# Attention plus gated FFN on one core: K's weights moved to another DMA queue, two crossbar tiles ranked earlier, one PSUM copy moved to ScalarE

## The chip, the cores and the metric

One core of a Trainium2 chip. The metric is the device time of one execution in us; smaller is better. The kernel before takes 517.59 us (median of 3 runs, 517.06 to 518.33).

## The reference, cut to what matters

```python
x = A_x                                  # (1, 2048, 576) bf16
xn = _layernorm(x)                       # mean, variance over 576
# A: linear attention, 32 heads of 18
qkv = xn @ wqkv                          # (576, 3*576)
phi = lambda t: where(t > 0, t + 1, exp(t)) + 1e-6
kv  = einsum("bhsd,bhse->bhde", phi(k), v);  z = sum over s of phi(k)
o   = (phi(q) @ kv) / (phi(q) . z + 1e-6) @ wo
# B: gated FFN, 4608 wide
return x + o + (gelu(xn @ w_gate) * (xn @ w_up)) @ w_down
```

The 2048 rows are 16 tiles of 128. The first stage (up to 70 us) makes, for each tile, the layernorm, its transpose, the K and Q projections, phi of both, and the sums G = xn^T phi(K). The rest (446 us) is mostly the FFN.

## The kernel before, the parts concerned

Loads at the start. SyncE and ScalarE each issue DMAs on a queue of their own (q1 and q10 in the profile):

```python
def load_w(which, on=nc.sync):           # which: 0 = Q, 1 = K, 2 = V
    c = slice(which * D, (which + 1) * D)
    on.dma_start(wqkv_sb[:, 0:4, c], A_wqkv[0:512, c].rearrange("(kt p) c -> p kt c", p=P))
    on.dma_start(wqkv_sb[0:HP, 4, c], A_wqkv[512:576, c])      # the tail, 64 rows

load_x(0, 1)                             # tile 0, SyncE
load_x(1, 1, nc.scalar)                  # tile 1, ScalarE
load_w(1, nc.scalar)                     # K
nc.scalar.preload_act_table_set("natural_log_exp_and_others")
load_x(2, 2)                             # tiles 2, 3
load_w(0)                                # Q
load_x(4, 4)
```

Tiles 0 and 1 are transposed by TensorE into PSUM and copied out; tiles 2 to 15 go through the DMA crossbar:

```python
def transposes(n, k0=0, k1=KT, b=None):  # TensorE
    for kt in range(k0, k1):
        nc.tensor.transpose(tp_bank(b)[:, kt, :], xn[:, n, kt * P:(kt + 1) * P], ident[:])
def dma_transposes(n):                   # DMA crossbar
    nc.sync.dma_start_transpose(xnT[:, :, n * P:(n + 1) * P], xn[:, n, 0:640])
```

A planner in the program fixes the order of instructions at build time. Each step has an engine, an assumed duration, a rank, the steps it needs, a `ready` time for loads and a `tail` until its result lands. It starts what can start earliest, and among what can start within 0.05 us takes the lowest rank. None of these numbers is work on the chip; they only order the instructions.

```python
X_AT = [3.50, 4.20, 6.50, 6.50] + [9.50] * 4
for n in range(NS):
    lead = {0: -9.0, 1: 0.5}.get(n, 0.0)
    ...
    step(("stats", n, h), "DVE", 0.41, n - 2.2 + lead, ...)
    step(("aggr", n), "DVE", 0.21, n - 2.1 + lead, ...)
    step(("rstd", n), "ACT", 0.49, n - 2.1 + lead, ...)
    if n < TD:                           # TD = 2: transposed by TensorE
        for i, (k0, k1, eng) in enumerate([(0, 3, "ACT"), (3, KT, "DVE")]):
            step(("norm", n, i), "DVE", ...); step(("tp", n, i), "PE", ...)
            step(("xnT", n, i), eng, 0.48 if eng == "ACT" else 0.30, n - 0.88 + lead, ...)
    else:                                # crossbar
        step(("norm", n), ...)           # ScalarE for odd tiles, VectorE for even ones
        step(("xnT", n), "SP", 2.10, n - 1.9, [("norm", n)], lambda n=n: dma_transposes(n), tail=0.6)
    # mm, exp, phi of K (rank n) and Q (rank n + 0.6) in halves; G (rank n + 1.15)
```

Of the kernel before, what the change touches and what calls it, by code (L numbers as in the profile page):

```python
# [8 lines left out]
ACT = mybir.ActivationFunctionType  # L9
# [6 lines left out]
P = 128  # L16
HP = 64
# [11 lines left out]
KT = 5  # L29
# [28 lines left out]
def kernel(  # L58
# [11 lines left out]
    nc = tc.nc  # L70
# [21 lines left out]
    def load_x(n0, cnt, on=nc.sync):  # L92
        on.dma_start(x_sb[:, n0:n0 + cnt, :], x_view[:, n0:n0 + cnt, :])
# [8 lines left out]
    wqkv_sb = apool.tile([P, KT, 3 * D], BF16, name="wqkv_sb")  # L102


    def load_w(which, on=nc.sync):
        c = slice(which * D, (which + 1) * D)
        on.dma_start(wqkv_sb[:, 0:4, c], A_wqkv[0:512, c].rearrange("(kt p) c -> p kt c", p=P))  # L107
        on.dma_start(wqkv_sb[0:HP, 4, c], A_wqkv[512:576, c])

    load_x(0, 1)  # L110
    load_x(1, 1, nc.scalar)
    load_w(1, nc.scalar)
    nc.scalar.preload_act_table_set("natural_log_exp_and_others")
    load_x(2, 2)
    load_w(0)
    load_x(4, 4)

# [18 lines left out]
    xnT = persist.tile([P, KT, S], BF16, name="xnT")  # L136
# [63 lines left out]
    def ln_half(n, h):  # L200
        if h == 0:
            ln_raw[n] = asmall.tile([P, 2, nc.vector.BN_STATS_DIM], F32, name="stats")
        nc.vector.bn_stats(out=ln_raw[n][:, h, :], in_=x_sb[:, n, h * HALF:(h + 1) * HALF])  # L203

    def ln_aggr(n):
        nc.vector.bn_aggr(out=mv[:, n, :], in_=ln_raw[n][:])

    def ln_rstd(n):
        r = rstd[:, n:n + 1]
        nc.scalar.activation(out=r, in_=mv[:, n, 1:2], func=ACT.Ln, bias=eps_ln[:], scale=1.0)  # L210
        nc.scalar.activation(out=r, in_=r, func=ACT.Exp, scale=-0.5)

    def ln_bias(n):
        nc.gpsimd.tensor_scalar(
            out=nbias[:, n:n + 1], in0=mv[:, n, 0:1], scalar1=rstd[:, n:n + 1], scalar2=-1.0, op0=ALU.mult, op1=ALU.mult,
        )

    def ln_norm_act(n):
        nc.scalar.activation(  # L219
            out=xn[:, n, 0:D], in_=x_sb[:, n, :], func=ACT.Identity, bias=nbias[:, n:n + 1], scale=rstd[:, n:n + 1],  # L220
        )

    def ln_norm(n, c0=0, c1=D):
        nc.vector.tensor_scalar(
            out=xn[:, n, c0:c1], in0=x_sb[:, n, c0:c1], scalar1=mv[:, n, 0:1], scalar2=rstd[:, n:n + 1],
            op0=ALU.subtract, op1=ALU.mult,
        )
# [8 lines left out]
    def transposes(n, k0=0, k1=KT, b=None):  # L236
        b = TP_BANK[n] if b is None else b
        for kt in range(k0, k1):
            nc.tensor.transpose(tp_bank(b)[:, kt, :], xn[:, n, kt * P:(kt + 1) * P], ident[:])

    def tp_copy(n, k0=0, k1=KT, b=None, copy=acopy):
        b = TP_BANK[n] if b is None else b
        copy(out=xnT[:, k0:k1, n * P:(n + 1) * P], in_=tp_bank(b)[:, k0:k1, :])

    def dma_transposes(n):
        nc.sync.dma_start_transpose(xnT[:, :, n * P:(n + 1) * P], xn[:, n, 0:640])
# [4 lines left out]
    def kq_mm(n, which, hf):  # L251
        c = which * D + hf * HALF
        for kt in range(KT):
            nc.tensor.matmul(  # L254
                ps_all[:, KQ_BANK[which] + hf, :HALF], lhsT=xnT[:, kt, n * P:(n + 1) * P],
                rhs=wqkv_sb[:, kt, c:c + HALF], start=(kt == 0), stop=(kt == KT - 1),
            )

    def kq_exp(n, which, hf):
        e = e_tiles[n, which, hf] = awork.tile([P, HALF], F32, name="phi_e", tag="phi_e", bufs=8)  # L260
        nc.scalar.activation(  # L261
            out=e[:], in_=ps_all[:, KQ_BANK[which] + hf, :HALF], func=ACT.Exp, bias=neg1[:], scale=1.0,
        )

    def kq_phi(n, which, hf):
        nc.vector.scalar_tensor_tensor(  # L266
            out=(pq, pk)[which][:, n, hf * HALF:(hf + 1) * HALF], in0=e_tiles[n, which, hf][:], scalar=1.0,
            in1=ps_all[:, KQ_BANK[which] + hf, :HALF], op0=ALU.min, op1=ALU.max,
        )
# [11 lines left out]
    def g_accumulate(n, pieces):  # L281
        for kt, ps_ in pieces.items():
            j0, m = (kt * P, P) if kt < 4 else (4 * P, HP + 1)
            for b, col, d0, w in ps_:
                nc.tensor.matmul(  # L285
                    ps_all[:m, b, col:col + w], lhsT=xn[:, n, j0:j0 + m], rhs=pk[:, n, d0:d0 + w],
                    start=(n == 0 and col == 0), stop=(n == NS - 1), skip_group_check=True,
                )
# [120 lines left out]
    def step(name, *args, **kw):  # L409
        steps[name] = _Step(*args, **kw)  # L410

    X_AT = [3.50, 4.20, 6.50, 6.50] + [9.50] * 4
    W_AT = {1: 5.50, 0: 7.60}

    for n0 in range(8, NS, 2):
        step(("x", n0), "SP", 0.50, n0 - 5.5, [], lambda n0=n0: load_x(n0, 2), ready=1.6 * n0 + 2.0, tail=3.0)
    for n in range(NS):
        lead = {0: -9.0, 1: 0.5}.get(n, 0.0)
        after_x = [("x", n // 2 * 2)] if n >= 8 else []
        x_at = X_AT[n] if n < 8 else 0.0  # L420
        for h in range(2):
            step(("stats", n, h), "DVE", 0.41, n - 2.2 + lead, after_x, lambda n=n, h=h: ln_half(n, h), ready=x_at)
        step(("aggr", n), "DVE", 0.21, n - 2.1 + lead, [("stats", n, 0), ("stats", n, 1)], lambda n=n: ln_aggr(n))
        step(("rstd", n), "ACT", 0.49, n - 2.1 + lead, [("aggr", n)], lambda n=n: ln_rstd(n))
        if n < TD:
            for i, (k0, k1, eng) in enumerate([(0, 3, "ACT"), (3, KT, "DVE")]):
                b = TP_BANK[n] - i
                step(("norm", n, i), "DVE", 0.25, n - 2.1 + lead, [("rstd", n)],
                     lambda n=n, k0=k0, k1=k1: ln_norm(n, k0 * P, min(k1 * P, D)))
                step(("tp", n, i), "PE", 0.20, n - 1.5 + lead, [("norm", n, i)],  # L430
                     lambda n=n, k0=k0, k1=k1, b=b: transposes(n, k0, k1, b))
                step(("xnT", n, i), eng, 0.48 if eng == "ACT" else 0.30, n - 0.88 + lead, [("tp", n, i)],
                     lambda n=n, k0=k0, k1=k1, b=b, eng=eng: tp_copy(n, k0, k1, b, acopy if eng == "ACT" else vcopy))
            ready = [("xnT", n, 0), ("xnT", n, 1)]
        else:
            if n % 2:
                step(("bias", n), "POOL", 0.15, n - 2.1, [("rstd", n)], lambda n=n: ln_bias(n))
                step(("norm", n), "ACT", 0.65, n - 2.1, [("bias", n)], lambda n=n: ln_norm_act(n))
            else:
                step(("norm", n), "DVE", 0.43, n - 2.1, [("rstd", n)], lambda n=n: ln_norm(n))  # L440
            step(("xnT", n), "SP", 2.10, n - 1.9, [("norm", n)], lambda n=n: dma_transposes(n), tail=0.6)
            ready = [("xnT", n)]
        for which, rank in ((1, n), (0, n + 0.6)):
            for h in range(2):
                r = rank + h / 100
                free = [("phi", n - 1, which, h)] if n else []
                step(("mm", n, which, h), "PE", 0.615, r, ready + free, lambda n=n, w=which, h=h: kq_mm(n, w, h),
                     ready=W_AT[which], tail=0.15)
                step(("exp", n, which, h), "ACT", 0.49, r + 0.10, [("mm", n, which, h)],
                     lambda n=n, w=which, h=h: kq_exp(n, w, h))  # L450
                step(("phi", n, which, h), "DVE", 0.44, r + 0.15, [("exp", n, which, h)],
                     lambda n=n, w=which, h=h: kq_phi(n, w, h))
        step(("G", n), "PE", 0.75, n + 1.15, [("phi", n, 1, 0), ("phi", n, 1, 1)], lambda n=n: g_accumulate(n, G_A))
# [42 lines left out]


    load_w(2)
    for i in range(NWBUF):
        load_gu(i, 0)  # L500
# [156 lines left out]
```

## Time and profile before

| | before |
|---|---|
| time, median of 3 | 517.59 us |
| span of the profiled run | 516.2 us |
| TensorE busy | 509.0 us (99%) |
| VectorE, ScalarE busy | 203.4, 136.9 us |
| first K matmul (L254) | 6.73 us |
| FFN's first matmul (L309) | 69.94 us |

TensorE's busy time says little, since matmuls overlap and their ends are modelled. What is read are starts: a step between two groups that is longer than the number of matmuls times their pace is a gap in which TensorE issued nothing. The prediction shows the lines of the TensorE timeline and of the chain of waits.

### The profile page before, as it was taken

The numbers are of one execution on the slowest core, as the hardware profiler recorded it, in microseconds if no ns is written. First come the engines' busy times: TensorE is split into PE (matmuls) and PEld (weight loads), VectorE is DVE, ScalarE is ACT, GpSimd is POOL, SyncE is SP. The second block draws the span as 40 slices with busy tenths as digits, with TensorE's granted clock in tenths as the row PEclk, the third lists the DMA queues.
The fourth block names the chain that finished last, engine by engine and source line by source line (L and its number), as shares of the span: only waits on it lengthen the run. The fifth ranks groups of instructions, "written<-read, shape, count | busy, mean of one in ns | idle before, by whom it ended". The sixth has DMA issues, their size and how long they took to land.

```text
span 516.2 us, 10568 instructions
## 1 busy us (share of the span) xinstructions
PE 509.0 (99%) x4487; PEld 308.6 (60%) x4487; DVE 203.4 (39%) x415; ACT 136.9 (27%) x266; POOL 8.3 (2%) x26
## 2 busy tenths in 40 slices
PE   7999999999999999999999999999999999999997
PEld 6778864444487744444677644444777544445775
DVE  6887447667501036766401133333101234333100
ACT  4888523223310023233100022322000133232000
POOL 3001000000000000000000000000000000000000
PEclk9999999999999999999999999999999999999999
DMA  7443919999900045666400155555100455540000
GB/s 206 103 96 65 251 39 224 286 285 270 235 30 13 13 141 149 175 181 166 133 11 20 55 154 158 158 143 156 33 15 13 126 157 144 158 120 2 13 11 24
DMA packets 118745, 61.02 MB, mean 118 GB/s; under 512 B 25514, under 2 KB 117866, under 8 KB 118698
## 3 DMA queue, kind: packets, MB, share of 16 engines
q1 hardware_dynamic: 117946, 59.54, 44.5%
q8 instruction: 35, 0.57, 0.5%
q10 hardware_dynamic: 752, 0.81, 0.5%
q14 instruction: 12, 0.10, 0.1%
HBM read 52.79 MB, written 2.36 MB: 107 GB/s over the span
## 4 chain that ended last, share of the span: by engine, by line
PE 95%; DMA 3%; ACT 1%; DVE 0%; ACTq 0%; issue 0%; SPq 0%
PE ps_all L309 54%; PE ps_all L604 27%; PE ps_all L254 6%; PE ps_all L609 4%; PE ps_all L285 3%; DMA xnT<-xn 2%; DMA wqkv_sb<-in_A_wqkv_dram 1%; ACT phi_e L261 0%; PE ps_all L356 0%; PE ps_all L586 0%; ACT xn L219 0%; DVE hT L576 0%; ACT gl L575 0%; DVE res L612 0%; ACTq L107 0%
## 5 line engine op out<-in xcount | busy, mean ns | idle before, releaser
L309 PE MATMUL ps_all<-xnT,wg 64*128 64x512 bf16 x1152 | 272.0, 376 | 0.0
L309 PE MATMUL ps_all<-xnT,wu 64*128 64x512 bf16 x1152 | 271.5, 376 | 0.0
L575 ACT ACTIVATE gl<-ps_all 128x512 f32<-128x512 f32 x144 | 86.0, 597 | 313.7 <-PE ps_all L309 313.7
L576 DVE TENSOR_TENSOR hT<-ps_all,gl 128x512 bf16<-128x512 f32 x144 | 99.2, 689 | 143.6 <-ACT gl L575 143.2
L309 PEld LDWEIGHTS <-wu 64*128 64x128 bf16 x1152 | 108.3, 94 | 68.2
L309 PEld LDWEIGHTS <-wg 64*128 64x128 bf16 x1152 | 108.3, 94 | 67.8
L604 PE MATMUL ps_all<-wd_sb,hT 128*128 128x288 bf16 x1152 | 147.1, 286 | 0.0
L604 PEld LDWEIGHTS <-hT 128*128 128x128 bf16 x1152 | 112.3, 98 | 30.0 <-issue 1.6
L612 DVE TENSOR_TENSOR res<-ps_all,x_sb 128x288 bf16<-128x288 f32 x32 | 14.6, 457 | 144.9 <-PE ps_all L609 144.9
L309 PE MATMUL ps_all<-xnT,wr 64*128 64x512 bf16 x288 | 54.7, 376 | 0.0
L254 PE MATMUL ps_all<-wqkv_sb,xnT 128*128 128x288 bf16 x320 | 42.5, 286 | 1.8 <-DMA xnT<-xn 1.0
L254 PEld LDWEIGHTS <-xnT 128*128 128x128 bf16 x320 | 30.3, 98 | 9.8 <-DMA xnT<-xn 1.7
L261 ACT ACTIVATE phi_e<-ps_all,neg 128x288 f32<-128x288 f32 x64 | 30.9, 496 | 10.5 <-PE ps_all L254 7.2
L609 PE MATMUL ps_all<-m_sb,pqT 126*128 126x288 bf16 (+1 forms) x160 | 24.9, 286 | 0.0
L309 PEld LDWEIGHTS <-wr 64*128 64x128 bf16 x288 | 14.0, 94 | 17.3 <-issue 0.7
L285 PE MATMUL ps_all<-hT,xn 128*128 128x288 bf16 (+4 forms) x176 | 22.6, 275 | 0.0
L285 PEld LDWEIGHTS <-xn 128*128 128x128 bf16 (+1 forms) x176 | 17.6, 101 | 3.9
L609 PEld LDWEIGHTS <-pqT 126*128 126x128 bf16 (+1 forms) x160 | 15.6, 97 | 4.1
L266 DVE SCALAR_TENSOR_TENSOR pq<-phi_e,ps_all 128x288 bf16<-128x288 f32 x32 | 14.1, 450 | 8.0 <-ACT phi_e L261 7.8
L266 DVE SCALAR_TENSOR_TENSOR hT<-phi_e,ps_all 128x288 bf16<-128x288 f32 x32 | 14.1, 448 | 3.4 <-ACT phi_e L261 3.3
L203 DVE BATCH_NORM_STATS2 stats<-x_sb 128x6 f32<-128x288 bf16 x32 | 13.5, 439 | 1.8 <-DMA x_sb<-in_A_x_dram 1.8
L388 DVE SCALAR_TENSOR_TENSOR pn<-pq,den_d 128x504 bf16<-128x504 bf16 (+1 forms) x32 | 13.1, 449 | 0.0
(52 smaller groups left out, 95.4 us busy)
## 6 DMA issues: line engine op xcount, KB each, us to landing
wg<-in_B_w_gate_dram SPq DMA_DIRECT2D x72, 256.0 KB, 2.9
wu<-in_B_w_up_dram SPq DMA_DIRECT2D x72, 256.0 KB, 3.5
wd_sb<-in_B_w_down_dram SPq DMA_DIRECT2D x12, 432.0 KB, 5.2
wr<-in_B_w_gate_dram SPq DMA_DIRECT2D x72, 32.0 KB, 2.7
wr<-in_B_w_up_dram SPq DMA_DIRECT2D x72, 32.0 KB, 3.1
out_dram<-res SPq DMA_DIRECT2D x15, 144.0 KB, 1.8
x_sb<-in_A_x_dram SPq DMA_DIRECT2D x5, 288.0 KB, 3.2
wqkv_sb<-in_A_wqkv_dram SPq DMA_DIRECT2D x2, 576.0 KB, 6.7
```

The source lines that it names most:

```text
L203: nc.vector.bn_stats(out=ln_raw[n][:, h, :], in_=x_sb[:, n, h * HALF:(h + 1) * HALF])
L254: nc.tensor.matmul(ps_all[:, KQ_BANK[which] + hf, :HALF], lhsT=xnT[:, kt, n * P:(n + 1) * P], rhs=wqkv_sb[:, kt, c:c + HALF], start=(kt == ...
L261: nc.scalar.activation(out=e[:], in_=ps_all[:, KQ_BANK[which] + hf, :HALF], func=ACT.Exp, bias=neg1[:], scale=1.0,)
L266: nc.vector.scalar_tensor_tensor(out=(pq, pk)[which][:, n, hf * HALF:(hf + 1) * HALF], in0=e_tiles[n, which, hf][:], scalar=1.0, in1=ps_al ...
L285: nc.tensor.matmul(ps_all[:m, b, col:col + w], lhsT=xn[:, n, j0:j0 + m], rhs=pk[:, n, d0:d0 + w], start=(n == 0 and col == 0), stop=(n == ...
L309: return nc.tensor.matmul(self.outs[i], lhsT=self.lhs(i, rows, kt), rhs=self.rhs(i, rows, kt), start=start, stop=stop, skip_group_check=True,)
L388: nc.vector.scalar_tensor_tensor(out=pn[:].rearrange("p (c t) -> p c t", t=P)[:, c0:c1, :nh * DH].rearrange("p c (h e) -> p c h e", e=DH), ...
L575: nc.scalar.activation(out=gl[:], in_=ps_all[:, b[0], :], func=ACT.Gelu_apprx_tanh)
L576: nc.vector.tensor_tensor(out=hT[:, GUB * k + i, :], in0=ps_all[:, b[1], :], in1=gl[:], op=ALU.mult)
L604: nc.tensor.matmul(acc, lhsT=hT[:, f, j * P:(j + 1) * P], rhs=wd_sb[:, f, hs], start=(f == 0), stop=False,)
L609: nc.tensor.matmul(acc, lhsT=pqT[:rows, c, ts_], rhs=m_sb[:rows, c, hs], start=False, stop=(c == NCH - 1),)
L612: nc.vector.tensor_tensor(out=res[:, hs], in0=acc, in1=x_sb[:, n, hs], op=ALU.add)
```

## The change

Its intent: let K's weights have the DMA engines to themselves right after the first tile, bring tile 2 to the crossbar sooner, and take a copy off VectorE, which is the fuller engine at the start.

```diff
-    def load_w(which, on=nc.sync):
+    def load_w(which):                        # always on SyncE's queue
     load_x(0, 1)
     load_x(1, 1, nc.scalar)
-    load_w(1, nc.scalar)
     nc.scalar.preload_act_table_set("natural_log_exp_and_others")
+    load_w(1)
     load_x(2, 2)
     load_w(0)
     load_x(4, 4)
@@
-    X_AT = [3.50, 4.20, 6.50, 6.50] + [9.50] * 4
+    X_AT = [3.65, 4.20, 6.40, 6.40] + [9.50] * 4
-        lead = {0: -9.0, 1: 0.5}.get(n, 0.0)
+        lead = {0: -9.0, 1: 0.5, 2: -0.5, 3: -0.5}.get(n, 0.0)
-            for i, (k0, k1, eng) in enumerate([(0, 3, "ACT"), (3, KT, "DVE")]):
+            for i, (k0, k1, eng) in enumerate([(0, 3, "ACT"), (3, KT, "ACT" if n else "DVE")]):
-                step(("xnT", n, i), eng, 0.48 if eng == "ACT" else 0.30, n - 0.88 + lead, ...
+                step(("xnT", n, i), eng, 0.30 if i else 0.48, n - 0.88 + lead, ...
-            step(("xnT", n), "SP", 2.10, n - 1.9, ..., tail=0.6)
+            step(("xnT", n), "SP", 2.10, n - 1.9, ..., tail=1.7)
```

More of the change, by code (lines that the diff above doesn't have):

```diff
@@ L102 @@
     wqkv_sb = apool.tile([P, KT, 3 * D], BF16, name="wqkv_sb")
-    def load_w(which, on=nc.sync):
+    def load_w(which):
         c = slice(which * D, (which + 1) * D)
-        on.dma_start(wqkv_sb[:, 0:4, c], A_wqkv[0:512, c].rearrange("(kt p) c -> p kt c", p=P))
-        on.dma_start(wqkv_sb[0:HP, 4, c], A_wqkv[512:576, c])
+        nc.sync.dma_start(wqkv_sb[:, 0:4, c], A_wqkv[0:512, c].rearrange("(kt p) c -> p kt c", p=P))
+        nc.sync.dma_start(wqkv_sb[0:HP, 4, c], A_wqkv[512:576, c])
     load_x(0, 1)
     load_x(1, 1, nc.scalar)
-    load_w(1, nc.scalar)
     nc.scalar.preload_act_table_set("natural_log_exp_and_others")
+    load_w(1)
     load_x(2, 2)
@@ L431 @@
                      lambda n=n, k0=k0, k1=k1, b=b: transposes(n, k0, k1, b))
-                step(("xnT", n, i), eng, 0.48 if eng == "ACT" else 0.30, n - 0.88 + lead, [("tp", n, i)],
+                step(("xnT", n, i), eng, 0.30 if i else 0.48, n - 0.88 + lead, [("tp", n, i)],
                      lambda n=n, k0=k0, k1=k1, b=b, eng=eng: tp_copy(n, k0, k1, b, acopy if eng == "ACT" else vcopy))
@@ L440 @@
                 step(("norm", n), "DVE", 0.43, n - 2.1, [("rstd", n)], lambda n=n: ln_norm(n))
-            step(("xnT", n), "SP", 2.10, n - 1.9, [("norm", n)], lambda n=n: dma_transposes(n), tail=0.6)
+            step(("xnT", n), "SP", 2.10, n - 1.9, [("norm", n)], lambda n=n: dma_transposes(n), tail=1.7)
             ready = [("xnT", n)]
```

## The prediction

> **What bounds the kernel now.** I read the page first: TensorE is busy 509.0 of 516.2 us and the chain that ended last is 95% TensorE, 3% DMA, 1% ScalarE. So only stretches in which TensorE issues nothing can be won, and they are few. I looked for them in the TensorE timeline of the first 60 us (start, duration, engine, line, operation, count, and in brackets the idle time with its releaser).
>
> ```profile
> 6.73 0.66 PE L254 MATMUL ps_all<-wqkv_sb,xnT 128*128 128x288 bf16 x4 [0.28 <-ACT xnT L243]
> 7.83 0.91 PE L254 MATMUL ps_all<-wqkv_sb,xnT 128*128 128x288 bf16 x6 [0.44 <-DMA wqkv_sb<-in_A_wqkv_dram]
> 8.57 0.44 PE L239 MATMUL ps_all<-ident,xn 128*128 128x128 bf16 x5
> 8.86 1.39 PE L254 MATMUL ps_all<-wqkv_sb,xnT 128*128 128x288 bf16 x10
> 10.08 0.91 PE L285 MATMUL ps_all<-hT,xn 128*128 128x288 bf16 x7
> 10.82 2.61 PE L254 MATMUL ps_all<-wqkv_sb,xnT 128*128 128x288 bf16 x20
> 14.40 1.40 PE L254 MATMUL ps_all<-wqkv_sb,xnT 128*128 128x288 bf16 x10 [0.96 <-DMA xnT<-xn]
> ...
> 29.17 2.92 PE L254 MATMUL ps_all<-wqkv_sb,xnT 128*128 128x288 bf16 x20
> 31.93 0.91 PE L285 MATMUL ps_all<-hT,xn 128*128 128x288 bf16 x7
> 32.68 2.61 PE L254 MATMUL ps_all<-wqkv_sb,xnT 128*128 128x288 bf16 x20
> ```
>
> The reader is to see starts, not ends (the ends are modelled and overlap). Twenty L254 matmuls followed without a wait take 2.45 us start to start (32.68 to 35.13), so one is 0.1225 us; seven L285 matmuls take 0.75. Hence the issue gaps: four matmuls from 6.73 end at 7.22, the fifth starts at 7.83: **0.61 us**. Twenty from 10.82 end at 13.27, the next starts at 14.40: **1.13 us**. The group at 29.17 lasts 2.92 where others last 2.61: **0.31 us**. From there to 70 us, and as far as I looked beyond, starts follow at the regular 3.2 us per tile. The three gaps sum to 2.05 us; before 6.73 TensorE waits for the first tile's transposed copy, which the change doesn't hasten. So about 2 us is all that this change can win.
>
> What releases each gap is in the chain of waits in order of time, first 36 us (start, length, what):
>
> ```profile
> 1.73 6.05 DMA wqkv_sb<-in_A_wqkv_dram
> ...
> 7.83 0.92 PE ps_all L254 x6
> 8.75 0.02 issue
> 8.78 0.50 ACT phi_e L261
> 9.28 0.19 ACT rstd L210
> 9.47 0.02 issue
> 9.49 0.21 ACT rstd L211
> 9.70 0.03 issue
> 9.73 0.44 DVE xn L224
> ...
> 10.24 4.11 DMA xnT<-xn
> ...
> 14.40 1.40 PE ps_all L254 x10
> ...
> 26.40 4.25 DMA xnT<-xn
> ```
>
> The first gap is the DMA issued at 1.73: the last 64 rows of K's weights (72 KB), landing at 7.78. That delay then runs through two exps, the rstd and the norm of tile 2 into its crossbar transpose, issued at 10.24 and landing only at 14.35: the second gap. The third is tile 7's transpose.
>
> **What the Trainium skill says.** "DMA: Bandwidth & Descriptors", section "Queues, rings and completion order": each DMA engine round-robins between the queue rows that it has work for, by packets, and consumes one row's ring in order. Section "Issuing engines are not separate DMA queues" adds that issuing from several engines saves only issue time. The DMA view agrees with the second: 387 GB/s in 5 to 6 us from two queues, 388 in 4 to 5 us almost from ScalarE's alone. With the first it agrees in that both rows move together, but not evenly. From 6 to 7 us (packets, MB, share of the 16 engines' time):
>
> ```profile
> q1 hardware_dynamic: 296, 0.34, 97.3%
> q10 hardware_dynamic: 48, 0.04, 12.3%
> ```
>
> Here q1 is SyncE's queue with Q's weights, q10 ScalarE's with the tail of K's; the small tail trickles beside a large transfer. "ScalarE: Activation LUTs", section "What ACT_TABLE_LOAD costs", gives 186 ns + 0.833 ns per element for an activation with immediate scale and bias; for 384 elements that is 506 ns, where the trace has 469 ns. "Runtime: NRT & Kernel Launch", section "Instruction fetch mechanics": instructions are refilled in 16 KiB blocks by DMA. The trace agrees: one instruction packet of 0.02 MB falls into 11 to 15 us and one into 27 to 31 us, just beside the two transposes that took 4.11 and 4.25 us; the others take 2.6 at the median.
>
> **The change, part by part.**
>
> 1. Queues. Before, SyncE issued x0, x2-3, Q's weights, x4-7, and ScalarE x1, K's weights. After, SyncE issues x0, K's weights, x2-3, Q's weights, x4-7, so K's 664 KB (in thousand bytes) no longer share. Estimate: x0 and x1 (147 KB each) are through at about 3.2 us, as now (x0 lands at 3.7). K's weights then take 664 / 387 GB/s = 1.7 us, to 4.9, and land some 0.5 us later, at about 5.4, before the first matmul at 6.73. The 0.61 us gap goes. x2-3 (295 KB) follow until 5.7 and land at about 6.2; the statistics of tile 2 start at 6.59, so they need not wait. Bytes up to the end of Q's weights are the same 1.92 MB in both kernels, so these land where they do now, 1.72 + 6.7 = 8.4 us.
> 2. What follows on TensorE: K of tile 0 from 6.73 to 7.95 (10 x 0.1225), the five transposes of tile 1 (about 0.3) by 8.3, then Q of tile 0 at 8.4 or a little later instead of 8.86. So Q's landing takes back some 0.15 us of the 0.61. If the transposes are ordered behind the first half of Q, it takes back 0.45.
> 3. Ranks. Only statistics, aggregate and rstd of tiles 2 and 3 get the half tile; norm and transposes keep their ranks. It matters in one place: tile 2's aggregate is done at 8.03, but its rstd waits behind two exps until 9.18. Ranked ahead, and with K's exps starting at about 7.5 instead of 8.16, one exp goes first (to 8.05), rstd takes 0.49 (to 8.55), norm 0.43 (to 9.0): the transpose is issued at about 9.05 instead of 10.24. With the median 2.6 us it lands at 11.7, with 4.1 at 13.2.
> 4. Tile 1's second copy leaves VectorE (0.28 us) and costs ScalarE about 0.37 (estimate: 469 less 128 x 0.833 ns of the skill's page). ScalarE then has exps of K, rstd, two copies before K of tile 1: 0.5 + 0.5 + 0.5 + 0.46 + 0.37 from 7.5 makes 9.8, when TensorE ends Q of tile 0 at 9.65. That may cost 0.2 us.
> 5. The longer tail (1.7 instead of 0.6) is no work on the chip: it makes the planner expect transposes later, so that it fills TensorE's order with the G sums first.
>
> Sum: without a wait TensorE needs from 6.73 to tile 2 10 + 10 + 20 matmuls, 5 transposes and a G sum, 4.90 + 0.30 + 0.75 = 5.95, so 12.7. Adding 0.15 for Q's weights and 0.2 for ScalarE's copies gives 13.05, against 14.40: 1.35 us won. Tile 2's transpose is there in the good case. Of the 1.35, I deduct 0.05 to 0.1 for smaller waits of the next tiles, whose exps and phis now follow closer, and leave tile 7's gap as it is. The rest of the kernel is bound by TensorE and moves forward as a whole: 517.59 less 1.3 is **516.3 us**.
>
> **The rivals.**
>
> - *The gap moves to the transposes.* Tiles 5 to 7 gate next: tile 5's transpose is issued at 21.23 and lands at 23.8, and TensorE needs it at about 24.0. Against: their norms wait in order behind phis that TensorE itself releases, so they move along. For: VectorE and ScalarE are busy 4.6 and 4.1 of 5 us from 10 to 15. If a gap of 0.6 to 1 us opens there, the time is 516.9 to 517.3.
> - *Everything hides.* If tile 2's transpose again meets an instruction fetch and Q's weights land late with the transposes behind them, only 0.3 to 0.5 us remain: 517.2.
> - *All three gaps close.* If tile 7's transpose, issued earlier, misses the fetch and the x loads, the gain is up to 1.7 to 2 us: 515.6 to 515.9.
> - *K's weights delay x2.* Were x2-3 to land at 7 instead of 6.2, statistics and the norm of tile 1 behind them slip 0.5 us; the loss would eat the first gap's gain, 517.
>
> **Range and chances.** The centre is 516.3. Closed gaps alone end at 515.5; the first two rivals reach 517.3, and the three runs before span 517.06 to 518.33. So 515.5 to 517.4 for 8 in 10. A change of 2% is 10.4 us, five times all gaps together: within 2% is nearly certain.
>
> **What would show it.** Right: no wait for K's weights at 6.73, ten matmuls in a row; K's tail landing before 6; tile 2's transpose issued near 9; K of tile 2 starting near 13; from there the same 3.2 us per tile. Wrong: a wait for x2-3 in VectorE's statistics, a first matmul later than 6.8, a wait for Q's weights over 0.3 us, or a new or longer gap at tiles 3 to 8 that gives back the lead, to be read off the start of the stage at 70 us.

## The result, and the profile after

The changed kernel takes 516.59 us (median of 6 runs, 516.39 to 518.57) against 518.04 for the kernel before in 6 runs. The ratio is 0.9977, 95% interval 0.9957 to 0.9997: within 2%, and a little faster. A ratio here and below is the mean time of one kernel's runs over that of the other's of the same rounds, so it is not quite the ratio of the medians quoted. By the ratio the gain is about 1.2 us (by its interval 0.2 to 2.2), by these medians 1.45. Five of the six runs lie between 516.39 and 516.85; one took 518.57, and nothing in its record says why.

The profile of the changed kernel, TensorE timeline (start, duration, engine, line, operation, count, idle time):

```profile
6.91 1.40 PE L254 MATMUL ps_all<-wqkv_sb,xnT 128*128 128x288 bf16 x10 [0.34 <-ACT xnT L243]
8.14 0.33 PE L239 MATMUL ps_all<-ident,xn 128*128 128x128 bf16 x3
8.31 0.78 PE L254 MATMUL ps_all<-wqkv_sb,xnT 128*128 128x288 bf16 x5
8.92 0.28 PE L239 MATMUL ps_all<-ident,xn 128*128 128x128 bf16 x2
9.03 2.00 PE L254 MATMUL ps_all<-wqkv_sb,xnT 128*128 128x288 bf16 x15
10.87 0.91 PE L285 MATMUL ps_all<-hT,xn 128*128 128x288 bf16 x7
11.62 2.61 PE L254 MATMUL ps_all<-wqkv_sb,xnT 128*128 128x288 bf16 x20
14.06 0.91 PE L285 MATMUL ps_all<-hT,xn 128*128 128x288 bf16 x7
...
27.60 2.61 PE L254 MATMUL ps_all<-wqkv_sb,xnT 128*128 128x288 bf16 x20
30.05 0.91 PE L285 MATMUL ps_all<-hT,xn 128*128 128x288 bf16 x7
```

From 6.91 on every start follows the one before at the regular pace: ten matmuls by 8.14 (1.23), fifteen from 9.03 to 10.87 (1.84, 0.1225 each), twenty from 11.62 to 14.06 (2.44). K of tile 2 is the second half of that twenty: it starts at 11.62 + 10 x 0.1225 = 12.85 instead of 14.40. **All three gaps are gone**, that of tile 7 too (27.60 to 30.05 is 2.45). Only the first matmul starts 0.18 later. That is within the spread of single executions: after_issue_late, below, with the same order up to there, has it at 6.71. The sum, 0.61 + 1.13 + 0.31 - 0.18 = 1.87 us, is what the start of the FFN shows: 68.06 instead of 69.94. The span is 514.5, 1.7 less; the other 0.2 us goes somewhere in the FFN and was not traced. Each profile is of one execution: the one before took 518.27 us, above the median of its kernel, the one after 516.39, the fastest of its six. The two lie 1.88 us apart, so the profiles show more gain than the medians and the ratio do.

The chain of waits after has no weights and no transposes in it; up to the first matmul it goes through x0 alone:

```profile
0.80 3.00 DMA x_sb<-in_A_x_dram
...
3.83 0.83 DVE stats L203 x2
...
6.37 0.49 ACT xnT L243
6.86 0.05 issue
6.91 1.40 PE ps_all L254 x10
```

The rest of the comparison, from the timelines: tile 2's rstd starts at 8.13 instead of 9.18, its crossbar transpose is issued at 9.20 instead of 10.24, and lands after 2.7 us instead of 4.11. So of the 2.47 us by which tile 2 is there sooner, 1.04 come from the issue and 1.43 from the transfer itself. The DMA view says what differed in the transfer. Before, from 11.5 to 14 us (queue, kind: packets, MB, share of the 16 engines' time):

```profile
DMA packets 673, 0.18 MB, mean 72 GB/s; under 512 B 672, under 2 KB 672, under 8 KB 672
...
q1 hardware_dynamic: 672, 0.16, 98.6%
q8 instruction: 1, 0.02, 2.4%
```

After, from 10.4 to 11.6 us:

```profile
DMA packets 672, 0.16 MB, mean 137 GB/s; under 512 B 672, under 2 KB 672, under 8 KB 672
...
q1 hardware_dynamic: 672, 0.16, 68.9%
```

Both windows hold the same 672 packets of one transpose (640 of 256 bytes, and 32 small ones of 4 bytes that write semaphores). In the kernel before, one packet of the instruction queue lies among them, and the transpose needs 2.23 us from its first packet to its last semaphore instead of 0.93. This became the question of the experiments.

### The profile page after: what moved, and what is told of

The parts are those of the page before. It is cut to its first block, busy times and chain, and to the rows that moved or that the text cites. A ratio compares the mean times of both kernels' runs of the same rounds, so it can differ in the third digit from the quotient of the medians.

```text
span 514.5 us, 10566 instructions
## 1 busy us (share of the span) xinstructions
PE 509.2 (99%) x4487; PEld 309.5 (60%) x4487; DVE 203.0 (39%) x414; ACT 136.7 (27%) x267; POOL 8.4 (2%) x26
## 4 chain that ended last, share of the span: by engine, by line
PE 98%; DVE 1%; DMA 1%; ACT 0%; issue 0%
PE ps_all L309 54%; PE ps_all L604 27%; PE ps_all L254 8%; PE ps_all L285 4%; PE ps_all L609 4%; DMA x_sb<-in_A_x_dram 1%; PE ps_all L356 0%; DVE stats L203 0%; PE ps_all L586 0%; DVE hT L576 0%; PE ps_all L239 0%; ACT gl L575 0%; ACT xnT L243 0%; DVE res L612 0%; DVE xn L224 0%
```

## The experiments

Two pairs of theories. **F**: a 16 KiB instruction fetch in flight together with a crossbar transpose holds it up, so that what counts is whether the two meet. **I**: only the moment of the transpose's issue counts. And **P**: the parts of the plan need one another, against "one part carries the gain". Each kernel below gave a correct result. "Gap" is computed from starts as above, and "FFN" is the start of the FFN's first matmul, both in the one profiled execution. Between profiles the first K matmul alone moves by 0.3 us (6.71 to 7.01 where no matmul was added ahead of it); the timed ratios have intervals of about plus or minus 0.0013 (0.7 us). A gap is read from the profile, then, and the ratio only says whether the time goes along.

| kernel | first K matmul | gap in K of tile 0 | gap at tile 2 | other gap | FFN | median us | ratio (95%) |
|---|---|---|---|---|---|---|---|
| before | 6.73 | 0.61 | 1.13 | 0.31 (tile 7) | 69.94 | 518.04 | 1 |
| after | 6.91 | none | none | none | 68.06 | 516.59 | 0.9977 (0.9957 to 0.9997) |
| queues_only | 6.96 | none | 0.87 | 0.21 (tile 7) | 69.20 | 517.23 | 0.9986 (0.9973 to 1.0) |
| plan_only | 6.93 | 0.33 | none | none | 68.42 | 516.91 | 0.9983 (0.997 to 0.9995) |
| before_fetch_early | 6.71 | 0.65 | 1.04 | none | 69.57 | 517.77 | 0.9998 (0.9985 to 1.001) |
| after_fetch_early | 7.22 | none | 0.60 | none | 69.08 | 517.18 | 0.9986 (0.9973 to 0.9998) |
| after_issue_late | 6.71 | none | 1.86 | none | 69.74 | 518.44 | 1.0018 (1.0003 to 1.0033) |
| before_issue_late | 6.86 | 0.40 | 2.42 | about 0.5 (tile 7) | 71.38 | 519.32 | 1.0021 (1.0009 to 1.0033) |
| ranks_only | 6.79 | 0.47 | none | 0.64 (K of tile 1) | 69.07 | 517.51 | 0.9991 (0.9978 to 1.0004) |
| copy_only | 6.86 | 0.59 | 1.56 | none | 70.21 | 518.51 | 1.0007 (0.9995 to 1.0019) |
| after_no_ranks | 6.88 | none | 1.65 | none | 69.74 | 517.23 | 0.9987 (0.9975 to 1.0) |
| after_no_copy | 6.83 | none | none | 0.64 (K of tile 1) | 68.64 | 517.24 | 0.9987 (0.9975 to 1.0) |
| after_no_tail | 7.01 | none | none | none | 68.17 | 516.58 | 0.9976 (0.9962 to 0.9989) |
| tail_only | 6.72 | 0.55 | 0.44 (G of tile 1) | none | 68.96 | 517.4 | 0.9992 (0.998 to 1.0005) |

The kernel before ran at 517.85 to 518.1 us (medians) beside these. Runs of one kernel spread by up to 2 us (copy_only: 517.09 to 519.11), as much as the gaps; whether the fetch met the transpose in the runs that were not profiled isn't known.

**queues_only**: the new queues with the old order.

```diff
-    load_w(1, nc.scalar)
     nc.scalar.preload_act_table_set("natural_log_exp_and_others")
+    load_w(1)
```

> The kernel before with the new queues alone (K's weights second on SyncE's queue, x1 alone on ScalarE's); the order of all engines' instructions stays as before. Theory F (an instruction fetch on one DMA engine holds up a crossbar transpose that is in flight): the 0.61 us gap goes, tile 2's transpose is issued near 9.8 instead of 10.24, its packets run from about 11.0 to 11.9, and TensorE's first instruction fetch comes near 11.5 because TensorE is 0.4 us further; so the transpose is again held up and lands near 13.8, the second gap stays at about 1 us, and the gain is only about 0.5 us: ratio 0.999. Rival theory I (only the moment of issue counts): it lands 2.6 us after its issue, at 12.4, no second gap, gain 1.5 us or more: ratio 0.997.

The first gap goes, ten matmuls run on from 6.96. The transpose of tile 2 is issued at 9.87 and takes 3.85 us, and 0.87 us of gap stays. The fetch came at 10.74, not at 11.5, and met the packets (11.16 to 13.12) all the same. F, not I.

**plan_only**: everything but the queues.

```diff
-    lead = {0: -9.0, 1: 0.5}.get(n, 0.0)
+    lead = {0: -9.0, 1: 0.5, 2: -0.5, 3: -0.5}.get(n, 0.0)      # and the copy, the tail, X_AT
```

> All of the change but the queues: ranks, longer tail, second copy on ScalarE, with K's weights still on ScalarE's queue. The 0.61 us gap for the tail of K's weights stays (fifth matmul of tile 0 at 7.8); tile 2's transpose is issued near 9.8, its packets are over by about 11.9. Theory F: the first fetch comes 0.4 us later than in the kernel after, near 12.3, and just misses it; it lands near 12.4, no second and no third gap, gain 1.3 to 1.5 us: ratio 0.9973. If the queues were what matters, the gain would be under 0.5 us.

K's weights still land at 7.70 and TensorE waits for them (0.33 us, since its first matmul came later). The transpose is issued at 9.55, its last semaphore is written at 11.76, the fetch starts at 12.12: no gap at tile 2 and none at tile 7. Of the 1.88 us at the FFN's start the plan alone brings 1.52, the queues alone 0.74; the two overlap. The new X_AT values, which are part of the plan, were not tried alone.

**before_fetch_early**: an attempt to move the fetch.

```diff
-NWARM = 38
+NWARM = 48
-    step(("spin",), "PE", 0.11, -1.0, [("tp", 0, 1)], lambda: spin(2))
+    step(("spin",), "PE", 0.11, -1.0, [("tp", 0, 1)], lambda: spin(6))
```

> The kernel before with 14 more warm-up matmuls in stretches in which TensorE waits anyway (48 instead of 38 at the start, 6 instead of 2 after the first transposes). No DMA, no order, no rank is changed; only TensorE's instruction count ahead of tile 2 is 28 higher, so that the 16 KiB fetch comes 14 matmuls earlier, near 10.2 instead of 11.90. Theory F: the fetch is over before tile 2's packets start at 11.5, the transpose issued at 10.24 lands at 12.9 instead of 14.35, the second gap (1.13 us) goes and the first (0.61) stays; gain 1.1 to 1.4 us, ratio 0.9975. Rival (the first crossbar transpose is slow by itself, or by the data): it still takes 4.1 us and nothing changes, ratio 1.000.

The lever didn't work: with 14 more warm-up matmuls ahead of it (28 instructions, since each has a weight load), the first fetch came at 11.83 instead of 11.90. The transpose took 4.03 us and the gap stayed. That settles nothing between the theories about the transpose. It speaks against my assumption that TensorE's instruction count sets the moment of the first fetch. (The third gap closed: the second fetch ran from 27.69 to 28.65, and tile 7 wasn't late for TensorE.)

**after_fetch_early**: the same with 42 and 8 in the kernel after.

> The kernel after with 10 more warm-up matmuls in stretches in which TensorE waits (42 instead of 38, 8 instead of 2), which moves the first fetch from 11.93 to about 10.7, into tile 2's packets (10.3 to 11.4). Theory F: the transpose takes 4 us instead of 2.7 and lands at about 13.2; TensorE needs it at about 13.0, so a gap of 0.2 to 0.5 us opens there: ratio to the kernel before near 0.9985 instead of 0.9977. Rival: the landing stays 2.7 us after the issue, and no gap opens.

The first fetch came at 11.71, not 10.7, and the added matmuls weren't free: the first K matmul came 0.31 us later. With that the transpose, issued at 9.50, had its packets from 10.79, and its end just touched the fetch. The packet records: 637 of the 640 data packets start by 11.72; the last three of 256 bytes start at 12.61 or later, when the fetch (11.71 to 12.63) ends. It landed 4.31 us after issue and a gap of 0.60 us opened. This fits F, with 0.01 us of overlap, though not by the move that I intended.

**after_issue_late and before_issue_late**: move the transpose instead of the fetch.

```diff
+        if n == 2:
+            for j in range(2):            # 3 in before_issue_late
+                nc.sync.dma_start(idle_sb[:, j, :], xn[0:16, 2, 0:D])   # read by nobody
         nc.sync.dma_start_transpose(xnT[:, :, n * P:(n + 1) * P], xn[:, n, 0:640])
```

> The kernel after, but SyncE issues two copies of 16 rows into a tile that nobody reads between the norm of tile 2 and tile 2's crossbar transpose, so that this is issued at about 10.3 instead of 9.20, as late as in the kernel before; nothing else is changed. Theory F (an instruction fetch that overlaps a transpose holds it up): its packets run from about 11.6 and meet the fetch that comes near 11.9; from the first packet to the last semaphore it takes 1.9 to 2.3 us instead of 0.93, it lands at about 14.3, TensorE needs it at 13.0, and a gap of 1.1 to 1.4 us opens: ratio about 0.9995. Theory I (only the moment of issue counts, 2.6 us to landing): it lands at 12.9, no gap, ratio 0.9977.

> The kernel before with three such copies ahead of tile 2's transpose: it is issued at about 11.9 instead of 10.24. Theory F: its packets start at about 13.2, after the fetch (11.9 to 12.8), run the undisturbed 0.93 us and it lands at about 14.5 to 14.7, only 0.2 to 0.3 us later than in the kernel before, though it was issued 1.6 us later; the time stays within 0.4 us of it. Theory I: it lands 1.6 us later, at 16.0, and the time grows by 1.6 us, ratio 1.003.

The chain of waits of after_issue_late:

```profile
10.26 4.19 DMA xnT<-xn
14.45 0.05 issue
14.50 1.40 PE ps_all L258 x10
```

And of before_issue_late:

```profile
12.81 2.74 DMA xnT<-xn
15.55 0.05 issue
15.60 1.40 PE ps_all L258 x10
```

Issued about one us later than in the kernel after, the transpose took 4.19 us instead of 2.7 (fetch 11.63 to 12.87, packets from 11.54); the gap is 1.86 us, larger than expected because TensorE was ready at 12.64. Issued 2.6 us later than in the kernel before, after the fetch (11.10 to 12.35) was over, it took 2.74 instead of 4.11. The issue came 0.9 us later than I had planned (the third copy held SyncE longer), so that it lands 1.2 us later than in the kernel before, not 0.2 to 0.3, and the time grows by 0.2%. What tells the theories apart is the duration, and it went as F says, in both directions. The idle copies don't hold the transpose up by themselves: three of them stand ahead of the quick one. The ratio of after_issue_late, 1.0018 where about 0.9995 was expected, is not all its gap. Two of its six runs took 520.3 us, 2 us more than the others, and their record has a granted TensorE clock of 0.996 where the other four have 1.0; 0.4% of 518 us is 2 us. Without the two its mean is 518.21, against 517.96 for the kernel before: a ratio of 1.0005.

**ranks_only**: the lead alone. The planner got one dependence more (tile 0's G after tile 1's copies). Without it, G of tile 0 is ordered ahead of tile 1's copies, whose transposes lie in the same PSUM banks; the memory check refused that order, also for the copy alone and for the kernel after without the ranks or without the copy. What the dependence does by itself was not run.

```diff
-    lead = {0: -9.0, 1: 0.5}.get(n, 0.0)
+    lead = {0: -9.0, 1: 0.5, 2: -0.5, 3: -0.5}.get(n, 0.0)
```

> The kernel before with the half-tile lead of tiles 2 and 3 alone, plus one dependence in the planner (tile 0's G sums after tile 1's copies, since they share PSUM banks; without it the check finds the sums overwriting tile 1's transposes). Tile 2's transpose is issued near 9.8 and its packets are over by about 12, just ahead of the fetch. But tile 1's second copy on VectorE now stands behind the statistics of tile 3: K of tile 1 waits for it until about 11.3, a new gap of about 1.2 us in place of the one at tile 2. Theory P (the parts need each other; the copy is moved because of this): gain under 0.5 us. Rival (the ranks alone carry the plan's gain): gain 1.2 us or more, ratio 0.9977 or less.

As expected in kind: tile 2 is in time (transpose issued at 9.55, undisturbed), but K of tile 1 waits for its copy on VectorE. TensorE timeline of ranks_only:

```profile
11.01 1.03 PE L254 MATMUL ps_all<-wqkv_sb,xnT 128*128 128x288 bf16 x7 [0.48 <-DVE xnT L243]
```

The bracket names the releaser: L243 on VectorE is that copy. The gap is 0.64 us, not 1.2, and the timed gain is not clear of nothing (0.9991, 0.9978 to 1.0004).

**copy_only**: the second copy on ScalarE alone (same dependence).

```diff
-    enumerate([(0, 3, "ACT"), (3, KT, "DVE")])
+    enumerate([(0, 3, "ACT"), (3, KT, "ACT" if n else "DVE")])
```

> The kernel before with tile 1's second copy on ScalarE alone, plus the same dependence. Tile 2's rstd still waits behind both exps of K, its transpose is issued near 10.2 and meets the fetch near 11.9: the first gap (0.6) and a second gap of about 1 us stay, gain 0 to 0.3 us. If the copy were what matters, K of tile 2 would start before 13.6.

The gap at tile 2 stays and is longer, 1.56 us: issue at 10.41, 4.52 us to landing, with the fetch at 12.59. Nothing is gained.

**after_no_ranks, after_no_copy, after_no_tail, tail_only**: one part taken out of the kernel after (the first two with the dependence), and the tail alone in the kernel before.

```diff
 # after_no_ranks: lead = {0: -9.0, 1: 0.5}.get(n, 0.0)
 # after_no_copy:  enumerate([(0, 3, "ACT"), (3, KT, "DVE")]), durations as before
 # after_no_tail:  tail=0.6        # tail_only: tail=1.7 in the kernel before
```

> The kernel after without the half-tile lead (with the planner's dependence of tile 0's G sums on tile 1's copies). Tile 2's rstd stands behind both exps of K again: the transpose is issued at 9.8 to 10.0 instead of 9.20, its packets run from about 11.2 to 12.1. Theory F: if the fetch comes between 10.2 and 12.1 it meets them, the landing is near 13.9 and a gap of about 1 us opens at tile 2 (gain 0.8 us, ratio 0.9985); the profile must show both or neither. Theory I: it lands at 12.5, no gap, ratio 0.9977.

> The kernel after with tile 1's second copy back on VectorE (with the same dependence). Theory P, as ranks_only showed: the copy stands behind statistics of tile 3, K of tile 1 waits for it until about 10.8, a gap of about 1.1 us there that names the copy, and none at tile 2; gain about 0.7 us, ratio 0.9986. Rival (the copy's engine doesn't matter): no gap there, ratio 0.9977.

> The kernel after with the planner's old 0.6 us instead of 1.7 us for the transposes' landing. The order of the first 15 us is the same by the plan, so no gap opens up to tile 3; only later orders of x loads and G sums can differ. Expected: no gap over 0.3 us, ratio within 0.0007 of the kernel after's 0.9977.

> The kernel before with the planner's longer landing alone: G of tile 1 goes ahead of K of tile 2 on TensorE. The first gap stays (0.6 us); the transpose of tile 2 is issued near 10.2 and meets the fetch as in the kernel before, landing at 14.3, but TensorE does G of tile 1 (0.75 us) meanwhile, as soon as its phis are there at about 13.8: the second gap shrinks from 1.13 to about 0.5 us. Gain about 0.6 us, ratio 0.9988.

*after_no_ranks*: issued at 9.84, data through by 12.05, gap 1.65 us. The DMA view from 12.2 to 13.5 us holds three packets in all:

```profile
DMA packets 3, 0.02 MB, mean 13 GB/s; under 512 B 2, under 2 KB 2, under 8 KB 2
...
q8 instruction: 1, 0.02, 4.5%
q1 hardware_dynamic: 2, 0.00, 0.2%
```

The one on q8 is the fetch (12.37 to 13.31). The two on q1 are the last two of the transpose's 32 semaphore writes. Thirty were done by 12.05, these two came at 13.29 and 13.30, as the fetch ended, and K of tile 2 started at 14.51. Two of 32 is the share of one of the 16 DMA engines, so a likely reading is that the transpose's work on that engine stood behind the fetch; the packet records don't name the engine. The same two records come at 29.44 and 29.45 for tile 7 in the kernel before (fetch 28.33 to 29.45): that is the third gap. (The timeline names VectorE's norm as releaser of the wait of after_no_ranks; the norm had long been done, and the DMA records show what was late.) The moment at which the fetch's record starts doesn't explain everything. Here it is 1.25 us after the transpose's first packet, and the two writes were overdue already. For tile 7 in five profiles (after, plan_only, copy_only, after_no_tail, tail_only) the fetch starts 1.05 to 1.23 us after the first packet, and that transpose was through in 0.93. What held the two writes up to 12.37 stays open.

*after_no_copy*: the copy's gap again, 0.64 us, on VectorE; tile 2 is in time.

```profile
10.58 1.03 PE L254 MATMUL ps_all<-wqkv_sb,xnT 128*128 128x288 bf16 x7 [0.48 <-DVE xnT L243]
```

*after_no_tail*: no gap, 516.58 us: the longer tail adds nothing once the rest is there. *tail_only*: TensorE does start G of tile 1 while tile 2's transpose, met by a fetch (11.06 to 12.46), is on its way; 0.44 us of gap is left instead of 1.13, as expected.

**All transposes together.** In the 14 profiles I took each crossbar transpose of tiles 2 to 15 from its first packet to its last semaphore, and whether a fetch of the instruction queue lay in that time:

```
                        count   shortest   median   longest (us)
no fetch in that time    161      0.92      0.93     1.08 but for seven: six of 1.12 to 1.24, one of 1.68
a fetch in that time      35      1.32      1.9      2.26
tile 2 alone: 0.93 in the 6 profiles where it missed the fetch,
              1.94 to 2.26 in the 8 where it met one
```

The two groups hardly overlap. Fetches are not the only thing that lengthens a transpose: the one of 1.68 (tile 6 of tail_only) and four of the six ran beside loads of x, the other two began within 0.11 us after a fetch. One caution: the hold-up itself lengthens the time in which a fetch is looked for. So take the first 0.93 us alone, which every transpose needs. In 33 of the 196 a fetch's record reaches into them, and all 33 took 1.32 us or more. Of the other 163 three did: that of 1.68, and tile 2 of after_no_ranks and tile 7 of before_issue_late, whose data was through before the fetch's record starts (1.25 and 1.29 us after the first packet).

## Why the prediction was right, point by point

The time was in the range: 516.3 predicted, 516.59 measured, a gain of 1.3 predicted against 1.2 by the ratio. The mechanism of the two large gaps was right; that the sum came so near is in part luck, as the steps show:

1. *K's weights no longer share; the first gap goes.* Right: no wait at the first matmul, here and in queues_only, while it stays with the old queues (plan_only, ranks_only, copy_only, tail_only). Their last semaphore write comes at 5.17 instead of 6.96; after_issue_late, where the profile has the landings, has them at 5.47 and 5.78, before 6 as predicted. Tiles 2 and 3 landed at 6.45 (predicted 6.2) and their statistics started at 6.70 without waiting. Not predicted: x0's statistics start 0.1 us later with the new queues, at 3.71 to 3.96 in six of seven profiles and at 3.66 in one, against 3.66 to 3.76 with the old; that is part of the 0.18 at the first matmul, which came at 6.91, later than the 6.8 that the prediction had named as a sign of being wrong. The uneven shares that the prediction reads in the window from 6 to 7 us (296 packets against 48) say little about taking turns: 12 of the 48 are semaphore writes, and the records don't name the DMA engine, so some engines may have had nothing of K left.
2. *Q's weights and ScalarE's copies take back 0.15 + 0.2 us.* Wrong, they took nothing. Q's weights landed at 8.06 (the last 64 rows at 8.27), not 8.4. The planner put the first half of Q between tile 1's two groups of transposes and K of tile 1 ahead of tile 0's G. ScalarE's copy of 256 columns took 382 ns (predicted 0.37; the sum given there makes 0.36), and both were done at 9.68, when TensorE came to K of tile 1.
3. *Ranks bring the issue from 10.24 to about 9.05.* Right: 9.20, and after_no_ranks shows 9.84 without them. They turn out to be worth more than the 0.64 us between: at 9.84 the transpose meets the fetch and 1.65 us are lost.
4. *2.6 us if it misses the instruction fetch, 4.1 if not.* Right for this tile, and now shown rather than guessed at: 2.7, and 4.19 when it was issued late on purpose. That it would miss the fetch was assumed as the good case and not worked out, so this part was luck: its last semaphore is written at 11.43, and the fetch starts at 11.93.
5. *The longer tail orders G sums first.* Not in the kernel after; only in tail_only.
6. *Tile 7's gap stays.* Wrong, the mis-sized term is 0.31 us: tile 7's last semaphore is written at 26.33, and the second fetch starts at 26.46. This was the third rival, "all three gaps close", and again a matter of 0.13 us. The errors of points 1, 2 and 6 (0.18 too little cost, 0.35 too much, 0.31 too little gain) leave the profile's gain at 1.88 us at the FFN's start. The timed gain, 1.2 us with an interval of 0.2 to 2.2, cannot tell 1.3 from 1.88; that its middle lies nearer to what was predicted than the terms deserve is luck.

What stays open: what sets the moment of a fetch (the first one started between 10.74 and 12.63 us in the 14 profiles, and more TensorE instructions ahead of it did not bring it forward by more than 0.22 us), how the fetch holds the transpose up on its DMA engine, and from when, why 0.3 to 1.2 us pass between the last semaphore record and TensorE's start after a disturbed transpose, and the slow single run of the kernel after (518.57). A kernel faster than the one after was not found: after_no_tail equals it.

## What to carry to other kernels

Look at a DMA whose time to landing differs between instances that move the same bytes, and at what else is in its window: here the same transpose took 2.6 or 4.1 us, and the queue to look at was the one that the program doesn't issue on. When TensorE is busy 99%, find its gaps from starts, and sum them before predicting: they bound the gain. Parts of a planned order work together: ranks alone gained 0.45 us by the median and not clear of noise, since they only moved the wait to the next thing in line, and the copy alone gained nothing.

## What the Trainium skill lacked or had wrong

- "Runtime: NRT & Kernel Launch", "Instruction fetch mechanics": crossing a 16 KiB boundary is said to be mostly hidden. Whether the fetching engine waits was not looked at, but other DMAs are not spared: a fetch (one packet of 0.9 to 1.45 us on the instruction queue) in the time of a crossbar transpose goes with a stretch of that from 0.93 to between 1.32 and 2.26 us, and with up to 1.65 us of TensorE's time at one tile (after_no_ranks). The page's count (256 instructions per block) fits TensorE as the fetching engine: 35 blocks x 256 = 8960, against its 4487 matmuls and as many weight loads; no run shows it directly.
- "DMA: Bandwidth & Descriptors", "DMA Transpose (X-bar)": the page has no time from issue to landing for a tile of this size. Here 128 rows of 640 bf16 take 2.6 us from SBUF to SBUF undisturbed. Nor does it say what a long packet of another queue costs a transpose (2.8 to 4.6 us from issue to landing here).
- "ScalarE: Activation LUTs", "What ACT_TABLE_LOAD costs": the page has no cost for ScalarE's COPY. Its 186 ns + 0.833 ns per element is for an activation and would give 506 and 399 ns for 384 and 256 elements; the copies, of bf16 from PSUM, took 460 to 478 and 382 ns in the kernels before and after.
